# Filling the natural-order weights by copies from SBUF to SBUF in place of a trip through DRAM, in a 2:4 sparse matmul

## The chip, the cores and the metric

One core of a Trainium2 chip. The metric is the device time of one execution in microseconds (us). Most executions of one kernel agree within 0.3%. PE is the matmul engine (TensorE), DVE is VectorE, ACT is ScalarE, SP is SyncE, which here only issues transfers.

## The reference

```python
B, S, D = 16, 512, 1024            # x: [16, 512, 1024], w: [1024, 1024], b: [1024], all bf16
wg  = w.reshape(G, 4, D)           # groups of four rows, G = D // 4
thr = second largest |wg| of each group and column
wp  = (wg * (|wg| >= thr)).reshape(D, D)      # 2:4 pruning
return einsum("bsd,df->bsf", x, wp) + b
```

That is a pruning of a 2 MB weight matrix and then one matmul of 8192 tokens (64 tiles of 128) by 1024 by 1024.

## The kernel before

The weights are loaded "packed": partition q holds the four rows 4q to 4q+3 of a half g of the rows, so that VectorE can compare the four rows of a group in one partition. The pruned weights `wp` come out in that packed order. There are six pieces (half of the rows, range of columns); the last two, pieces 4 and 5, are the right half of the columns.

```python
wp     = const.tile([P, G, 4, Dout], bf16)     # packed: [q, g, m, f], row = 512 g + 4 q + m
wp_nat = const.tile([P, KT, Dout], bf16)       # natural: [p, kt, f],  row = 128 kt + p
scratch = dram.tile([D, Dout], bf16, name="wp_scratch")
scr_pk  = scratch.rearrange("(g q m) f -> q g m f", g=G, m=4)
scr_nat = scratch.rearrange("(kt p) f -> p kt f", p=P)
```

The first seven token tiles ("packed tiles") are multiplied against `wp` as it is: TensorE transposes their x tile in a matching order, and their matmuls fill the time in which VectorE is still pruning. The other 57 tiles ("natural tiles") use x tiles that a transposing load brings in natural order, and so need `wp_nat`. Before the change the pruned weights reach it by way of DRAM:

```python
def save(g, c0, c1, eng="sp"):                 # SBUF -> DRAM
    issue(eng, scr_pk[:, g, :, c0:c1], wp[:, g, :, c0:c1])
def reload(h):                                 # DRAM -> SBUF, column half h
    fs = slice(h * FH, (h + 1) * FH)
    sp(nc.sync.dma_start(wp_nat[:, :, fs], scr_nat[:, :, fs]))
# ... in ACT's order: "... S0 S3 W5 W4", where W saves pieces 5 and 4 (the right half)
run({eng: order[eng].split() for eng in order})
save(0, 0, 256); save(0, 256, 512); save(1, 0, 256); save(1, 256, 512)   # four lines in the file
load_batch(0)            # transposing load of the first natural batch, 5 tiles
reload(0)
reload(1)
load_batch(1)            # second natural batch, 4 tiles
load_batch(2)            # 8 tiles, as all later ones
for t in (2, 0, 3, 1, 6, 5, 4):
    finish(t)
# natural batch 0: the left column half of all its tiles first, then the right half;
# later batches: both halves of a tile at once
```

SP works through its issues in this order, and a `reload` waits until the `save`s that it reads have landed.

## Time and profile before

| | before |
|---|---|
| time, median of the first 3 runs | 235.51 us (235.48 to 235.56) |
| span in the profile | 233.2 us |
| PE busy | 229.5 us, 98% |
| first natural matmul | 33.46 us |
| second natural batch starts | 50.72 us |

First the page of the kernel before: busy time by engine, and the chain that ended last, which is followed backwards from the end of the execution, with its shares by engine and by line (L394 and L359 are the natural matmuls, L219 the packed ones).

```profile
span 233.2 us, 2871 instructions
## 1 busy us (share of the span) xinstructions
PE 229.5 (98%) x1184; PEld 112.8 (48%) x1184; DVE 104.2 (45%) x177; ACT 15.2 (7%) x27; POOL 0.7 (0%) x6
...
## 4 chain that ended last, share of the span: by engine, by line
PE 98%; DVE 0%; issue 0%
PE ps L394 76%; PE ps L219 10%; PE ps L359 9%; PE ps L131 2%; PE tp L194 2%; DVE o L363 0%; DVE zeros L80 0%
```

The list of waits of PE in the kernel before (total us, how often, longest):

```profile
engine line waited for: us in total, times, longest us
PE ps L131 <- DVE zeros L80: 1.0, 1, 1.0
```

A busy share alone would prove little: each of these matmuls is on record as 379 ns long although one starts every 216 ns, so the records overlap and the engine looks busy. The list of waits, which has one entry in the first microsecond and no other, and the chain, which is PE nearly from end to end, say it better: after the first microsecond TensorE never waits for anything.

Next SP's own queue in time (start, duration of the issue, what is issued; a merged row covers several issues and the waits between them), and the start of the natural matmuls on PE.

```profile
start us, us, engine line op out<-in xcount [idle before <-releaser]
...
10.55 6.84 SPq L92 DMA_DIRECT2D wp_scratch<-wp  x4
17.45 5.87 SPq L244 DMA_TRANSPOSE xb<-in_x_dram  x1
23.50 9.10 SPq L184 DMA_DIRECT2D wp_nat<-wp_scratch  x2
32.64 12.07 SPq L244 DMA_TRANSPOSE xb<-in_x_dram  x1
```

```profile
33.46 17.43 PE L359 MATMUL ps<-wp_nat,xb 128*128 128x512 bf16 x80
50.72 1.46 PE L394 MATMUL ps<-wp_nat,xb 128*128 128x512 bf16 x6
```

The DMA view, asked for one short stretch at a time, gives the time from one issue to its landing (last column). These are the reload of the right half, issued at 32.22, and the transposing load of the second batch, issued at 32.64:

```profile
issues: line engine op xcount, KB each, median us to landing
wp_nat<-wp_scratch SPq DMA_DIRECT2D x1, 1024.0 KB, 6.7
...
xb<-in_x_dram SPq DMA_TRANSPOSE x1, 16.6
```

The right half is complete at 38.9 us; TensorE asks for it after five groups of eight matmuls of 216 ns, at about 42.1. The second batch is complete at 32.64 + 16.6 = 49.2 us, and TensorE asks for it at 50.7. Everything arrives in time, the second batch with 1.5 us to spare.

### The profile page before, as it was taken

To read this page: it belongs to the slowest core of one execution; us is meant where nothing else is said; L and a number is where in the kernel's file an instruction comes from. 1 tells how busy PE (TensorE), PEld (TensorE's weight loads), DVE (VectorE), ACT (ScalarE), POOL (GpSimd) and SP (SyncE) were. 2 spreads that over 40 slices of the span, in tenths; PEclk is the share of its full clock that TensorE was granted. 3 is DMA by queue.
4 is the path that set the end of the run, shared out by engine and by line. 5 is a ranking of instruction groups with operands and counts; after the bars stand their busy time and mean duration, and the time that the engine had idled before them with its cause. 6 is when DMAs were issued, how large, how long until landed. Compare 5 with 4: busy or idle time off the path is not lost.

```text
span 233.2 us, 2871 instructions
## 1 busy us (share of the span) xinstructions
PE 229.5 (98%) x1184; PEld 112.8 (48%) x1184; DVE 104.2 (45%) x177; ACT 15.2 (7%) x27; POOL 0.7 (0%) x6
## 2 busy tenths in 40 slices
PE   8999999999999999999999999999999999999995
PEld 5987444444444444444444444444444444444443
DVE  3999559533343244244234334334324424423434
ACT  3679000000000000000000000000000000000000
POOL 1000000000000000000000000000000000000000
PEclk9999999999999999999999999999999999999999
DMA  6999969999999952992239921697221221122122
GB/s 189 297 327 248 322 214 224 282 257 247 241 340 258 273 166 88 209 285 94 90 74 253 257 91 46 146 239 202 90 90 49 88 93 63 72 90 91 47 89 90
DMA packets 79500, 40.29 MB, mean 173 GB/s; under 512 B 60416, under 2 KB 71936, under 8 KB 79488
## 3 DMA queue, kind: packets, MB, share of 16 engines
q1 hardware_dynamic: 68208, 22.32, 43.9%
q10 hardware_dynamic: 11280, 17.80, 22.9%
q8 instruction: 9, 0.15, 0.3%
q14 instruction: 3, 0.02, 0.0%
HBM read 6.29 MB, written 18.87 MB: 108 GB/s over the span
## 4 chain that ended last, share of the span: by engine, by line
PE 98%; DVE 0%; issue 0%
PE ps L394 76%; PE ps L219 10%; PE ps L359 9%; PE ps L131 2%; PE tp L194 2%; DVE o L363 0%; DVE zeros L80 0%
## 5 line engine op out<-in xcount | busy, mean ns | idle before, releaser
L394 PE MATMUL ps<-wp_nat,xb 128*128 128x512 bf16 x816 | 176.3, 379 | 0.0
L394 PEld LDWEIGHTS <-xb 128*128 128x128 bf16 x816 | 79.8, 98 | 96.3
L363 DVE TENSOR_TENSOR o<-ps,bias_sb 128x512 bf16<-128x512 f32 (+1 forms) x116 | 74.0, 677 | 117.2 <-PE ps L394 110.8
L219 PE MATMUL ps<-wp,xt 128*128 128x256 bf16 (+1 forms) x168 | 25.5, 308 | 0.0
L359 PE MATMUL ps<-wp_nat,xb 128*128 128x512 bf16 (+2 forms) x112 | 21.1, 349 | 0.0
L219 PEld LDWEIGHTS <-xt 128*128 128x128 bf16 x168 | 16.2, 98 | 7.5
L359 PEld LDWEIGHTS <-xb 128*128 128x128 bf16 x112 | 10.4, 98 | 10.7
L233 DVE TENSOR_TENSOR o<-ps,bias_sb 128x512 bf16<-128x512 f32 x7 | 4.8, 685 | 5.1 <-PE ps L219 5.1
L131 PE MATMUL ps<-zeros 128*128 128x128 bf16 (+1 forms) x32 | 5.3, 328 | 1.0 <-DVE zeros L80 1.0
L154 ACT ACTIVATE mag<-w_sb 128x1024 bf16<-128x1024 bf16 (+1 forms) x4 | 6.0, 1488 | 1.0 <-DMA w_sb<-in_w_dram 1.0
L151 DVE TENSOR_TENSOR wp<-w_sb,mag 128x1024 bf16<-128x1024 bf16 (+2 forms) x7 | 5.4, 766 | 0.2
L151 DVE TENSOR_TENSOR mag<-mag,hi 128x1024 bf16<-128x1024 bf16 (+2 forms) x7 | 5.3, 767 | 0.2
L199 ACT COPY xt<-tp 128x256 f32<-128x256 f32 x14 | 4.9, 372 | 5.3 <-PE tp L194 5.3
L194 PE MATMUL tp<-ident,x 128*128 128x128 bf16 x56 | 5.0, 227 | 0.0
L234 DVE TENSOR_TENSOR o<-st,bias_sb 128x512 bf16<-128x512 f32 x7 | 4.8, 679 | 0.0
L131 PEld LDWEIGHTS <-zeros 128*128 128x128 bf16 x32 | 3.0, 125 | 2.6 <-issue 1.7
L194 PEld LDWEIGHTS <-x 128*128 128x128 bf16 x56 | 4.0, 117 | 0.4 <-DMA x<-in_x_dram 0.2
L228 ACT COPY st<-ps 128x512 f32<-128x512 f32 x7 | 3.6, 609 | 0.1
L151 DVE TENSOR_TENSOR hi<-mag 128x512 bf16<-128x512 bf16 (+1 forms) x6 | 3.0, 507 | 0.0
L151 DVE TENSOR_TENSOR lo<-mag 128x512 bf16<-128x512 bf16 (+1 forms) x6 | 3.0, 508 | 0.0
L161 DVE TENSOR_SCALAR mag<-w_sb 128x1024 uint16<-128x1024 uint16 x2 | 0.9, 427 | 2.9 <-DMA w_sb<-in_w_dram 2.9
L151 DVE TENSOR_TENSOR hi<-hi,lo 128x256 bf16<-128x256 bf16 (+1 forms) x6 | 2.0, 336 | 0.2
(11 smaller groups left out, 6.4 us busy)
## 6 DMA issues: line engine op xcount, KB each, us to landing
out_dram<-o ACTq DMA_DIRECT2D x58, 256.0 KB, 3.9
wp_nat<-wp_scratch SPq DMA_DIRECT2D x2, 1024.0 KB, 6.4
x<-in_x_dram SPq DMA_DIRECT2D x5, 256.0 KB, 5.0
out_dram<-o ACTq DMA_DIRECT2D x10, 128.0 KB, 1.7
w_sb<-in_w_dram SPq DMA_DIRECT2D x4, 256.0 KB, 4.3
w_sb<-in_w_dram SPq DMA_DIRECT2D x2, 512.0 KB, 7.1
wp_scratch<-wp SPq DMA_DIRECT2D x4, 256.0 KB, 5.6
wp_scratch<-wp ACTq DMA_DIRECT2D x2, 512.0 KB, 5.2
```

Of the source, the lines that this page charges most:

```text
L131: pe(nc.tensor.matmul(warm_ps[:, :rep * P], lhsT=zeros[:], rhs=zeros[:, None, :].to_broadcast([P, rep, P]), start=True, stop=True))
L151: dve(nc.vector.tensor_tensor(out, a, b_, op=op))
L154: act(nc.scalar.activation(self.mag[:], self.w, Act.Abs))
L194: pe(nc.tensor.transpose(tp[:, m, :], xg[:, m, :], ident[:]))
L199: act(nc.scalar.copy(xt[:].bitcast(fp32), xpk[(t, g)][:].bitcast(fp32)))
L219: pe(nc.tensor.matmul(ps[:, c0 - h * FH:c1 - h * FH], lhsT=xpk[(t, g)][m], rhs=wp[:, g, m, c0:c1], start=(new and m == ms.start), stop=(le ...
L228: act(nc.scalar.copy(st[:], ps_open.pop((t, 0))[:]))
L233: dve(nc.vector.tensor_tensor(o[:, FH:], ps_open.pop((t, 1))[:], bias_sb[:, FH:], op=Alu.add))
L234: dve(nc.vector.tensor_tensor(o[:, :FH], staged.pop(t)[:], bias_sb[:, :FH], op=Alu.add))
L359: pe(nc.tensor.matmul(ps, lhsT=xt[:, kt, :], rhs=wp_nat[:, kt, c0:c1], start=(kt == 0), stop=(kt == KT - 1)))
L363: dve(nc.vector.tensor_tensor(o[:, c0:c1], ps, bias_sb[:, c0:c1], op=Alu.add))
L394: pe(nc.tensor.matmul(pss[h][:], lhsT=xt[:, kt, :], rhs=wp_nat[:, kt, h * FH:(h + 1) * FH], start=(kt == 0), stop=(kt == KT - 1)))
```

## The change

The intent is to fill the natural weights directly. A natural block of 128 rows is 32 partitions of the packed layout times their four rows, so one copy with 32 source partitions of 4 x 512 elements and 128 destination partitions of 512 elements puts the rows in place. Four copies serve a half of the rows and a half of the columns; sixteen serve all.

```diff
         elif tok[0] == "W":
-            save(*pieces[int(tok[1:])], eng="act")
+            pass
@@
-    save(0, 0, 256)
-    save(0, 256, 512)
-    save(1, 0, 256)
-    save(1, 256, 512)
+    def spread(g, h, eng="sp"):
+        fs = slice(h * FH, (h + 1) * FH)
+        for k in range(4):
+            issue(eng, wp_nat[:, 4 * g + k, fs], wp[32 * k:32 * k + 32, g, :, fs])
+
+    spread(0, 0)
     load_batch(0)
-    reload(0)
-    reload(1)
+    spread(1, 0)
+    spread(0, 1)
+    spread(1, 1)
     load_batch(1)
     load_batch(2)
```

## The prediction

> **What bounds the kernel now.** TensorE, almost without a gap. The page's busy line gives PE 229.5 of a 233.2 us span (98%), granted clock 1.00; PE's list of waits holds one entry, 1.0 us at the very start. The chain of waits is PE from 0.99 to 230.5 us (80 matmuls of the first natural batch take 17.27 us, 216 ns each), then 0.3 us of DVE and a last store. A change to data movement can gain at most the few us at the two ends, which it doesn't touch. It can only lose, by making PE wait.
>
> **Where the route through DRAM lies.** From issues and landings in windows of the DMA view, against PE's needs in the timeline:
> - Four saves issued by SP from 10.6 to 17.4 us; then the transposing load of the first natural batch, issued 17.45 (5.9 us of issue), landed 26.8.
> - Reload of the left half: issued 23.5 after an 8.2 us wait for saves, landed 29.5. PE's first natural matmul starts at 33.46: slack 4.0 us.
> - Right half: saves from ACT at 26.0 and 26.6, reload issued 32.2, landed 38.9, needed at 42.1: slack 3.2 us.
> - Transposing load of the second batch: issued 32.64, 16.6 us to land, 49.2; needed at 50.7. Slack 1.5 us, the tightest.
> All of this is off the critical path.
>
> **What the change does.** It removes 2 MB written to and 2 MB read from DRAM (six saves, two reloads) and two completion waits in a row (save landed, then reload issued). It adds 16 SP copies of 128 KB, 128 rows of 1 KB. Issuing a save cost SP 0.51 to 0.71 us; I estimate 0.5 to 0.6 per copy, 8 to 10 us in all. The Trainium skill ("DMA: Bandwidth & Descriptors", "Why a DMA increments its semaphore by 16 and not by 1") says the engine count is the largest up to 16 that divides the slowest dimension of both sides: 32 source and 128 destination partitions give 16, so the copies should not crawl on a few engines. No trace here shows that yet.
>
> Estimated new times: first four copies issued 10.5 to 13.5; first batch's transposing load at about 14 (was 17.45), landed 23.5; second four copies issued 20 to 22.5, landed by 26 (needed 33.46); third four 22.5 to 25; the last four wait for the last DVE multiply, which ends at 26.0: issued 26.0 to 28.5, landed about 31 (needed 42.1). The second batch's load is issued at about 29 (was 32.64), so its slack grows from 1.5 to about 5 us. Every deadline is met with more room.
>
> **Predicted time.** 235.5 us, unchanged; 8 times in 10 between 235.1 and 236.2. Faster by over 2%: 0.01; within 2%: 0.95; slower by over 2%: 0.04.
>
> **What would show each step.** PE busy 229 to 230 us, no wait of PE in the middle, first natural matmul at 33.4 to 33.5 us. SP issues of 0.5 to 0.6 us, copies landing in 2 to 6 us. First transposing load issued near 14, second near 29. Span unchanged.
>
> **What would make it wrong.** The copies running on few engines, so that the second four land after 33.46 or hold the second batch's load past 34 us; issues costing SP over 1 us each; an ordinary copy that waits for a transposing load on the same queue to end; stores on ACT held back by the larger number of copies in flight until output buffers run out and PE stops.

## The result, and the profile after

The changed kernel took 235.59 us (median of 4 runs, 235.52 to 235.82), the kernel before beside it 235.53 (4 runs, 235.48 to 235.65). The ratio is 1.0003, with a 95% interval of 0.9986 to 1.0021. Ratios here are not quite the ratio of the medians quoted. Kernels are compared only within the same rounds.

The page of the changed kernel. Its line numbers are shifted by three: L397 and L362 are the natural matmuls.

```profile
span 233.7 us, 2857 instructions
## 1 busy us (share of the span) xinstructions
PE 228.1 (98%) x1164; PEld 112.4 (48%) x1184; DVE 104.4 (45%) x177; ACT 15.2 (7%) x27; POOL 0.7 (0%) x6
...
## 4 chain that ended last, share of the span: by engine, by line
PE 96%; DMA 2%; issue 1%; SPq 1%; DVE 0%
```

1164 matmul records against 1184 weight loads means that 20 records are missing from this trace. They explain the missing 1.4 us of PE busy time at least in part and most of the "issue" share, so neither is a finding. The 2% of DMA in the chain is a load of x in the first 7 us. The waits of PE:

```profile
PE ps L131 <- DVE zeros L80: 1.0, 1, 1.0
PE tp L194 <- DMA x<-in_x_dram: 0.9, 2, 0.6
```

SP's queue, and PE's natural matmuls (80 in the first batch, of which one record is missing; the second row is cut off where the stretch that was asked for ends):

```profile
11.20 2.62 SPq L92 DMA_DIRECT2D wp_nat<-wp  x4
14.05 6.90 SPq L244 DMA_TRANSPOSE xb<-in_x_dram  x1
21.06 8.47 SPq L92 DMA_DIRECT2D wp_nat<-wp  x12
29.57 6.76 SPq L244 DMA_TRANSPOSE xb<-in_x_dram  x1
```

```profile
34.03 17.43 PE L362 MATMUL ps<-wp_nat,xb 128*128 128x512 bf16 x79
51.30 1.03 PE L397 MATMUL ps<-wp_nat,xb 128*128 128x512 bf16 x4
```

And the landings, for the stretch in which the last copy and the second batch's load are issued:

```profile
wp_nat<-wp SPq DMA_DIRECT2D x1, 128.0 KB, 3.0
xb<-in_x_dram SPq DMA_TRANSPOSE x1, 10.8
```

| us from the span's start | before | after |
|---|---|---|
| first batch's load issued, landed | 17.45, 26.8 | 14.05, 22.9 |
| left half complete (needed 33.46, 34.03) | 29.5 | 27 at the latest |
| right half complete (needed about 42.1, 42.7) | 38.9 | 31.9 |
| second batch's load issued, landed (needed 50.7, 51.3) | 32.64, 49.2 | 29.57, 40.4 |

So the transfers got a great deal more room: 10.9 us in place of 1.5 for the second batch. The time did not move. The 0.5 us between the two profiled spans is not of the change: in the chain the first packed matmuls start at 7.17 us before and 7.82 after, ahead of the first changed instruction at 11.2, because a load of x landed later in that execution. The profiled execution of the kernel before (234.98 us) was itself 0.5 us faster than its timed runs.

### The profile page after: what moved, and what is told of

Same layout as the page of the kernel before. It is cut to its first block, busy times and chain, and to the rows that moved or that the text cites. A ratio compares the mean times of both kernels' runs of the same rounds, so it can differ in the third digit from the quotient of the medians.

```text
span 233.7 us, 2857 instructions
## 1 busy us (share of the span) xinstructions
PE 228.1 (98%) x1164; PEld 112.4 (48%) x1184; DVE 104.4 (45%) x177; ACT 15.2 (7%) x27; POOL 0.7 (0%) x6
## 4 chain that ended last, share of the span: by engine, by line
PE 96%; DMA 2%; issue 1%; SPq 1%; DVE 0%
PE ps L397 75%; PE ps L219 10%; PE ps L362 9%; DMA x<-in_x_dram 2%; PE tp L194 1%; SPq L92 1%; PE ps L131 0%; DVE o L366 0%
## 5 line engine op out<-in xcount | busy, mean ns | idle before, releaser
L397 PE MATMUL ps<-wp_nat,xb 128*128 128x512 bf16 x800 | 175.4, 379 | 0.8
L397 PEld LDWEIGHTS <-xb 128*128 128x128 bf16 x816 | 79.9, 98 | 96.3
L362 PE MATMUL ps<-wp_nat,xb 128*128 128x512 bf16 (+2 forms) x110 | 21.0, 348 | 0.1
L362 PEld LDWEIGHTS <-xb 128*128 128x128 bf16 x112 | 10.4, 98 | 10.7
```

The costliest lines, as they stand in the source:

```text
L362: pe(nc.tensor.matmul(ps, lhsT=xt[:, kt, :], rhs=wp_nat[:, kt, c0:c1], start=(kt == 0), stop=(kt == KT - 1)))
L397: pe(nc.tensor.matmul(pss[h][:], lhsT=xt[:, kt, :], rhs=wp_nat[:, kt, h * FH:(h + 1) * FH], start=(kt == 0), stop=(kt == KT - 1)))
```

## The experiments

The main theory, **A**: TensorE sets the time, both routes are hidden under it, and a transfer costs nothing until it misses the moment at which TensorE asks for it. **Rival B**: the copies do save time and give it back through their sixteen issues and the DMA engines they occupy. **Rival C**: the room seen in the landing times is not a real difference between the routes.

### No route at all (e1_no_route)

```diff
-    spread(0, 0)   (and the three others)
-                rhs=wp_nat[:, kt, c0:c1]
+                rhs=wp[:, kt // 4, kt % 4, c0:c1]      # and the same in the other natural loop
```

> Wrong result on purpose: the natural matmuls read the packed weights where they lie, so no copy of any kind is made between the last DVE multiply and TensorE. Theory A (the whole route was hidden under TensorE in both kernels, so no route can be worth anything): 235.4 to 235.8 us, ratio to before 0.999 to 1.001, PE's list of waits without an entry in the middle. Rival B (the sixteen copies save time but give it back, in SP issues and in DMA engines taken from other transfers, so that the two cancel): a kernel with neither route is faster than both, by 0.5 us or more.

Measured: 235.47 us (6 runs) against 235.64 (11 runs), ratio 1.0003, interval 0.9988 to 1.0017; the result is wrong. PE's list of waits is this one line:

```profile
PE ps L131 <- DVE zeros L80: 1.0, 1, 1.0
```

A kernel without any copy is as fast as both. Rival B falls: there is nothing to give back. This is the largest gain that any route could have, and it is zero within 0.2%.

### Each copy twice, and three times (e4_copies_twice, e5_copies_thrice)

```diff
             issue(eng, wp_nat[:, 4 * g + k, fs], wp[32 * k:32 * k + 32, g, :, fs])
+            for _ in range(1):          # 2 in the other kernel
+                issue(eng, again[:, next(turn) % 12, :], wp[32 * k:32 * k + 32, g, :, fs])
```

> Each of the sixteen copies is issued a second time, into a scratch tile nobody reads: 32 copies. Theory A (threshold: free until a landing misses its deadline): 16 more issues of 0.6 us put the second batch's load from 29.6 to about 39 us, landing 50 to 53 against a need at 51.3; the last right-half copy lands near 42 against 42.6. So 235.5 to 237.5 us. Rival B (every copy costs TensorE its share at once): a rise of at least 1 us, and twice that rise when the copies are issued three times.

> Each copy issued three times, 48 copies. Theory A: first batch's load issued near 19, landed 28.5; left-half copies of the second half of k issued to 33, landed 36 against 34 (2 us of wait); last copies issued to 48, landed 51 against about 44.6 (6 us more); second batch's load issued at 48, landed about 60 (1 to 2 us more). In all 243 to 247 us, far more than twice the rise of the kernel with two of each. Rival B: exactly twice the rise of the kernel with two of each.

Measured: 241.96 us with two (ratio 1.0292, interval 1.0261 to 1.0324) and 254.98 us with three (1.0832, 1.0797 to 1.0867). The rises of the medians over 235.64 are 6.3 and 19.3 us, 3 to 1, where Rival B asked for 2 to 1. But theory A's numbers were too low in both. The waits of PE with two of each, and the same execution in stretches (PE busy, weight loads, granted clock, DMA share, GB/s, counting only the instructions that read the natural x tiles; a DMA share over 1 means that the recorded times of packets overlap):

```profile
PE ps L402 <- DMA xb<-in_x_dram: 3.8, 1, 3.8
```

```profile
50.00:55.00 5.00, 1.16 (x7) 0.32 (x5) 1.00 1.22 178
55.00:57.00 2.00, 2.00 (x6) 0.81 (x7) 0.58 1.27 290
57.00:59.00 2.00, 2.00 (x7) 0.71 (x5) 0.57 1.28 290
59.00:61.00 2.00, 2.00 (x11) 0.88 (x9) 1.00 1.29 329
```

The mechanism is the expected one: the second batch's load was issued at 39.23, as expected near 39, and TensorE waited for it, once. Two sizes were off. The load took 15.7 us to land, not 11 to 14, so the wait was 3.8 us. And a wait of that length has a price of its own: for the next 4 us the granted clock was 0.57 to 0.58 on average, with 6 or 7 matmuls in 2 us in place of 11, which costs about 1.9 us more (9 matmuls of 0.216 us). The wait and this loss make 5.7 us; that execution took 240.91 us, 5.3 more than the kernel before. The Trainium skill describes such a clock ("TensorE: Matmul & The Clock Gate", "What's actually happening": half rate after an idle window of about 3.4 us, full rate again after a busy one). The trace agrees: in stretches of half a microsecond the clock was 0.50 from 55.5 to 58.5 us and 1.00 again from 59.0, while after a wait of only 0.5 us (e11, below) it stayed at 1.00. With three of each PE waited 7.6 us for copies and 7.1 us for the second batch, and the clock fell to 0.50 in both waits. Why the load took 15.7 us at 39 us and 10.8 at 30 was not isolated.

### The same bytes on one DMA engine (e6_31_and_1)

```diff
-            issue(eng, wp_nat[:, 4 * g + k, fs], wp[32 * k:32 * k + 32, g, :, fs])
+            issue(eng, wp_nat[:124, 4 * g + k, fs], wp[32 * k:32 * k + 31, g, :, fs])
+            issue(eng, wp_nat[124:, 4 * g + k, fs], wp[32 * k + 31:32 * k + 32, g, :, fs])
```

> Each copy is cut into one of 31 source partitions (124 rows) and one of one source partition (4 rows): the same bytes, 32 issues, result still right. If the number of DMA engines is the largest up to 16 that divides the slowest dimension of both sides, the large piece runs on one engine, since 31 is prime[...], so the second group of copies lands near 50 us, the last near 85 to 95, and TensorE waits 45 to 65 us in all: 280 to 300 us. If rows are spread over engines whatever their number: as with 32 whole copies, 235.5 to 237.5 us.

Measured: 302.28 us (one run, state unknown), result right. PE waited 49.3 us for copies, eleven times, and 7.4 us for the first batch, whose load the slow copies held back on SP: 56.7 us in all, inside the 45 to 65 that were expected, though the time lies a little above its range. A stretch of 5 us within them shows what the DMA engines did (last three columns: granted clock, mean share of 16 engines, GB/s):

```profile
PE ps L363 <- DMA wp_nat<-wp: 49.3, 11, 6.0
```

```profile
45.00:50.00 5.00, 0.61 (x1) 0.10 (x1) 0.00 (x0) 0.00 (x0) 0.00 (x0) 0.50 0.07 25
```

A share of 0.07 is one engine of sixteen (1/16 is 0.0625), at 25 GB/s, and the matmuls that each wait for the next copy start 5.3 us apart (47.38, 52.68, 57.97 us). The rule that the prediction leaned on holds here: 31 and 124 rows leave one engine. With 32 and 128 rows the changed kernel's copies kept a share of 0.74 at 177 GB/s from 25 to 30 us, where little else was moving. Against 32 whole copies (241.96 us) the same number of issues cost 60 us more, a lower clock in the waits included.

### Asking sooner: batches of 3 and 6 in place of 5 and 4 (e2_before_3_6, e3_after_3_6)

The change moved landing times, not the time. To see whether that room is real, both kernels were made to need the data sooner:

```diff
-        nb = min((5, 4)[len(batches)] if len(batches) < 2 else 8, NT - t0)
+        nb = min((3, 6)[len(batches)] if len(batches) < 2 else 8, NT - t0)
```

> The kernel before with the first natural batches of 3 and 6 tiles in place of 5 and 4: TensorE now needs the right half at about 38.6 us and the second batch at about 43.8 us. Theory A (the route through DRAM held the second batch's load back to 49 us and was free only because nothing asked for it sooner): the load, now of 6 tiles and still issued near 32.6 behind the right half's reload, lands at 50 to 52 us, TensorE waits 6 to 8 us, 241 to 244 us. Rival C (landing times have nothing to do with the route, so the changed kernel has no more room than this one): the same loss in both kernels of this pair.

> The same batch sizes of 3 and 6 in the changed kernel. Theory A (sixteen copies let the second batch's load be issued at 29.6 with nothing large ahead of it): it lands at 42.5 to 44.5 us against a need at 43.8 to 44.4: 235.5 to 236.5 us, 5 us or more under the kernel before with the same sizes. Rival C: as the kernel before with the same sizes, within 1 us.

Measured: the kernel before 243.58 us (ratio 1.0372 to its own form with 5 and 4, interval 1.0337 to 1.0407); the changed kernel 235.63 us (1.0002, 0.9985 to 1.0019). In the kernel before PE waited 5.8 us, once, for the second batch; in the changed kernel it did not wait for it. PE's wait, and the landing of the second batch's load in the kernel before and in the changed one:

```profile
PE ps L394 <- DMA xb<-in_x_dram: 5.8, 1, 5.8
xb<-in_x_dram SPq DMA_TRANSPOSE x1, 18.5
xb<-in_x_dram SPq DMA_TRANSPOSE x1, 13.8
```

The second batch's load was issued at 32.26 and landed 18.5 us later, at 50.8; in the changed kernel it was issued at 29.41 and landed 13.8 us later, at 43.2, with TensorE asking at 44.7. Rival C falls. The room is real, and worth about 8 us where it is asked for.

### Which part gives the room (e11_right_copied_3_6, e12_left_copied_3_6)

Both keep the sizes 3 and 6. In the first the left column half goes through DRAM and the right half is copied; in the second it is the other way round.

```diff
 # e11, from the kernel before             # e12, from the kernel before
-    save(...) of pieces 4, 5 on ACT      -    the four saves of pieces 0 to 3
-    reload(1)                            +    spread(0, 0)
+    spread(0, 1)                         -    reload(0)
+    spread(1, 1)                         +    spread(1, 0)
```

> One part alone, batches of 3 and 6: the left half still goes through DRAM, the right half is filled by eight copies. Theory A (the room comes from the right half alone, whose reload waited until 32 us for its saves and then lay ahead of the second batch's load): that load is issued near 28.5 and lands at 42 to 43.5 against a need near 44.5: no wait, 235.5 to 236 us. Rival (the left half's reload is what matters, or only all sixteen copies together): 240 us or more.

> The other part alone, batches of 3 and 6: the left half by eight copies, the right half through DRAM. Theory A: the reload of the right half is issued at 31 to 32 us as before and the second batch's load after it, landing near 50 against 44.5: 5 to 6 us of wait, 241 to 244.5 us, like the kernel before with these sizes. Rival: 235.5 to 237 us.

Measured: 235.99 us with the right half copied (ratio 1.0009, 0.9961 to 1.0056) and 243.75 us with the left half copied (1.0327, 1.0276 to 1.0377). The room comes from the right half. PE's waits for the second batch, in this order:

```profile
PE ps L400 <- DMA xb<-in_x_dram: 0.5, 1, 0.5
PE ps L396 <- DMA xb<-in_x_dram: 3.6, 1, 3.6
```

In the first, the second batch's load was issued at 30.23 and landed after 14.4 us, 0.5 us late (issue near 28.5 and no wait were expected); in the second it was issued at 32.02 behind the reload and landed after 17.1. The wait there was 3.6 us and not the expected 5 to 6, in part because PE came to its first natural matmul only at 35.09 us in that execution.

### One megabyte ahead of the load (e8_after_3_6_1mb_ahead)

```diff
     spread(1, 1)
+    ahead = wtmp.tile([P, KT, FH], bf16, name="ahead")
+    issue("sp", ahead[:], w.rearrange("(kt p) f -> p kt f", p=P)[:, :, :FH])
     load_batch(1)
```

> The changed kernel with batches of 3 and 6, and one load of 1 MB from DRAM, 128 rows of 8 pieces of 1 KB, put on SP just before the second batch's load; nobody reads it. Theory D (the second batch's load landed 18.5 us after its issue in the kernel before and 13.8 us in the changed one because a 1 MB reload was ahead of it on the DMA engines): the load is issued near 30.0 and lands near 48 against a need at 44.8; TensorE waits 3 to 4 us and restarts at a lower clock, 240 to 242 us. Rival (the later issue and the stores that it meets made it slower, the reload did not): landing at 44 to 45.5 us, 235.5 to 236.5 us.

Measured: 241.69 us (239.86 to 243.07, ratio 1.0244, interval 1.0167 to 1.0321: slower, though not surely by 2%). PE waited 4.4 us for the second batch. The landings:

```profile
ahead<-in_w_dram SPq DMA_DIRECT2D x1, 1024.0 KB, 6.5
...
xb<-in_x_dram SPq DMA_TRANSPOSE x1, 19.0
```

The load was issued only 0.55 us later than without the extra megabyte (29.96 against 29.41) and took 19.0 us in place of 13.8. Theory D holds: a 1 MB transfer just ahead costs the load 5.2 us, enough for the whole 4.7 us by which the same load was slower in the kernel before (18.5 against 13.8). The time is lost in the issue itself: SP was busy issuing this load for 14.9 us, 14.3 in the kernel before with these sizes, and 8.3 in the changed kernel without the extra megabyte.

### Changing the order alone (e7_before_3_6_load_first, e10_after_3_6_load_first)

If the place behind the reload is the trouble, putting the load first should cure the route through DRAM as well.

```diff
 # e7, from the kernel before, 3 and 6     # e10, from the changed kernel, 3 and 6
     reload(0)                                 spread(0, 1)
+    load_batch(1)                        +    load_batch(1)
     reload(1)                                 spread(1, 1)
-    load_batch(1)                        -    load_batch(1)
```

> The kernel before with batches of 3 and 6, route through DRAM kept, but the second batch's transposing load is put ahead of the right half's reload on SP. Theory A' (the loss of the kernel before with these sizes, 5.8 us of wait, came from the place of the load in SP's order, behind a reload that waits until 32 us for its saves, and not from DRAM as such): the load is issued near 22 us and lands at 36 to 39; the reload, issued near 32, lands at 38 to 40 against a need at 38.6 to 39.6; 0 to 1 us of wait, 235.5 to 237.5 us. Rival (only copies from SBUF to SBUF give the room): 241 us or more, as without the new order.

Measured: 246.9 us (ratio 1.0475, interval 1.0402 to 1.0548), worse than without the cure. Theory A' fell. The landings (first the stretch from 25 to 29 us, then the reload of the right half) and PE's wait:

```profile
wp_scratch<-wp ACTq DMA_DIRECT2D x2, 512.0 KB, 14.3
xb<-in_x_dram SPq DMA_TRANSPOSE x1, 22.8
...
wp_nat<-wp_scratch SPq DMA_DIRECT2D x1, 1024.0 KB, 6.4
```

```profile
PE ps L359 <- DMA wp_nat<-wp_scratch: 9.2, 1, 9.2
```

The right half's saves, issued by ACT at about 26 us, now took 14.3 us to land. In e2, with the same batches in the old order, they took 4.1 us beside the same reload of the left half; what is new beside them is the transposing load. The reload of the right half could only be issued when they had landed, at 41.88 in place of 31.84. Not all of the wait is their doing: SP was itself busy issuing the load until 36.27 (14.0 us, from 22.23), so with prompt saves the reload, at 6.4 us, would, as an estimate from these figures, still have landed near 42.7 against a need at 39.1. That leaves about 3.6 of the 9.2 us to the place in SP's queue, which the expectation had overlooked, and 5.6 to the late saves. The route has two hops, and the second starts only where the first ends. So a copy with one hop was tried in the same order:

> The changed kernel with batches of 3 and 6, and the second batch's transposing load put on SP ahead of the last four copies: the same turn of order that cost the route through DRAM 9.2 us of wait, because there its saves took 14.3 us to land beside the load and the reload had to follow them. Theory E (each transfer issued beside a transposing load is late, and the route through DRAM pays that twice, a copy once): the load is issued near 25, the last copies near 31 to 33 and land near 38 to 42 against a need at 39; 1 to 4 us of wait, 236.5 to 241 us, clearly under the 246.9 us of the route through DRAM in that order. Rival (copies inside SBUF aren't held up by a transposing load): no wait, 235.5 us. Rival (any transfer behind it waits for all of it to land): over 245 us.

Measured: 235.47 us (ratio 0.9985, interval 0.9948 to 1.0022), with no entry for a copy or for a natural x tile in PE's list of waits. The load, issued at 25.75, landed after 9.7 us. The last four copies, issued from 32.51 to 34.39, landed after 3.1, 3.4, 3.7 and 6.2 us. The last of them:

```profile
wp_nat<-wp SPq DMA_DIRECT2D x1, 128.0 KB, 6.2
```

It landed at 40.6. It fills the last of the eight row blocks, which TensorE first asks for at about 40.5 in the right half; that matmul started at 40.68, 0.39 us after the one before it in place of 0.22. So the room was used up to within 0.2 us. Theory E had the landing of the last copy right (38 to 42) and the wait wrong, because it took 39, when the first block is needed, for the deadline of all four. Nor does this run show that a transposing load does not hold copies up, as its rival had it: SP was busy issuing the load until 32.41, so the copies were issued only when the load had 3 us left. Why the fourth took 6.2 us was not isolated. What the pair shows is that the same order costs the route with two hops 9.2 us of wait and the route with one hop almost nothing. Of the two hops only the first, the saves, was late in e7; the reload took its usual 6.4 us.

### Can the room be turned into time? (e9_after_six)

Each packed tile costs TensorE eight transposes, which a natural tile does not need.

```diff
-    NPK = 7
+    NPK = 6
-        nb = min((5, 4)[len(batches)] ...
+        nb = min((5, 5)[len(batches)] ...
 (one tile's tokens taken out of the three orders and its loads, the others renumbered)
```

> Can the room be turned into time? The changed kernel with six packed tiles in place of seven, batches of 5 and 5: one tile less is transposed on TensorE (8 transposes, 0.45 us). If room in the transfers were what set the number of packed tiles: 235.1 us. But the packed matmuls of the first four pieces then end about 1.7 us before the multiply of the first right-half piece does at 21.0 us, so TensorE should wait there for VectorE: 235.5 - 0.45 + 1.7, that is 236.3 to 237.3 us.

Measured: 237.32 us (4 runs, 237.20 to 237.82; ratio 1.0068, interval 1.0010 to 1.0126), at the upper end of what was expected. PE's wait in the middle:

```profile
PE ps L218 <- DVE wp L150: 2.3, 2, 1.9
```

TensorE waited 1.9 us at 21.2 for VectorE's multiply of piece 4, and 0.5 us for that of piece 5. So with this order of work the number of packed tiles is set by VectorE's pruning, which ends near 26 us, and not by the transfers; other orders with six tiles were not tried. No version that beats both kernels came out.

## Why the prediction was right

**The time.** Predicted 235.5 us, 235.1 to 236.2; measured 235.59. Its main step, that TensorE bounds the kernel and the route is off the critical path, is shown directly by the kernel with no route (235.47 us).

**The copies.** Issues were predicted at 0.5 to 0.6 us; they took 0.54 to 1.36, median 0.605. Landings were predicted at 2 to 6 us; they took 2.6 to 6.2, median 3.3. The first batch's load was issued at 14.05 and landed at 22.9 (predicted 14 and 23.5), the second at 29.57 (predicted 29). The rule on the number of engines, from the Trainium skill ("DMA: Bandwidth & Descriptors", "Why a DMA increments its semaphore by 16 and not by 1"), was not shown by any trace at the time; the split into 31 and 1 partitions now shows it, and shows (in one run) that breaking it costs some 60 us beyond what the same number of whole copies costs.

**The room.** "Its slack grows from 1.5 to about 5 us" was the mis-sized term: the slack grew to 10.9 us. Of the 9.4 us of growth, 3.1 come from the earlier issue (3.6 were predicted), 0.6 from the later need in that execution, and 5.8 from the landing time. The step that failed is this landing time, which was carried over from the kernel before as 16.6 us and was 10.8. It held a wait behind the 1 MB reload just ahead, which the change removes: of the 5.8 us, 5.3 are time that SP no longer spends in the issue (6.8 us in place of 12.1). With batches of 3 and 6, one megabyte put back brings the wait back (19.0 against 13.8 us); with the real sizes this was not run. The error was harmless because it lay on the safe side.

**A line of the trace read wrongly.** The prediction has the left half's reload issued "after an 8.2 us wait for saves". That wait is the right half's: SP issued the first reload at 23.50, right after the transposing load, whose issue ended at 23.3, and then waited 8.2 us before the second at 32.22. So it was the right half, and not the left, that waited for its saves.

**The first natural matmul.** Predicted at 33.4 to 33.5 us, measured at 34.03. The step failed, but for a reason outside the change: the shift was there before the changed instructions began, and the kernel before with batches of 3 and 6 reached it at 34.51, also without the copies.

**What would make it wrong.** The conditions listed were not fulfilled, apart from one issue over 1 us (1.36), which delayed nothing that TensorE asked for. Two of them were made to happen in experiments, too few engines and a late second load, and each then cost time in the way described.

## What to carry to other kernels

Ask first what could be gained by the best conceivable form of a change: a wrong-result kernel that leaves the step out altogether answers that in one run, and here the answer was nothing. A transfer that is hidden has a deadline, and its price has a threshold: nothing up to the deadline, then the wait itself and, where the wait was 3.6 us or more in these runs, some 2 to 5 us of work at half the matmul clock. The room that a change like this one buys is still worth knowing, because it decides whether the next change (other batch sizes, another order) is free or costs 3%; and a landing time read from a trace belongs to what was in flight ahead of it, so it must not be carried over when that is removed.

## What the Trainium skill lacked or had wrong

- "TensorE: Matmul & The Clock Gate", "Back-to-back issue gap", gives about 131 ns per matmul for a sustained stream of weight loads and matmuls of 512 columns, and says that the single-matmul figure of about 216 ns over-counts there. This case shows such a stream at 17.27 us for 80, 216 ns each, at a granted clock of 1.00. The measurement agrees with the figure that the page calls an over-count.
- "DMA: Bandwidth & Descriptors", "Issuing engines are not separate DMA queues", calls the sequencer's time to issue usually small relative to the transfer. For the transposing loads it was not: 5.9 us of 9.4 for the first batch's load and 12.1 of 16.6 for the second's before, 6.9 of 8.9 and 6.8 of 10.8 after. On one queue that time delays everything behind.
- No page has a time for a small copy from SBUF to SBUF issued from SP: of the sixteen of 128 KB in 128 rows, twelve took 2.6 to 4.2 us from issue to landing, and the first four, issued while loads were in flight, 5.3 to 6.2.
- The same DMA page says in "Rules for kernel authors" that a transpose next to ordinary DMAs needs nothing. That is about correctness; for time, saves of 512 KB issued beside a transposing load and a 1 MB reload took 14.3 us to land (e7), and 4.1 beside the reload alone (e2).
- The rule of the same page on the number of engines held: 31 source and 124 destination partitions ran at a DMA share of 0.07 and 25 GB/s, one engine of sixteen.
